# Block-sparse attention and a gated feed-forward on one core: new orders on all engines, with five edits of layout and casts

## The chip, the cores and the metric

The kernel runs on one core of one Trainium2 chip. Five engines work side by side, each through its own list of instructions in order: TensorE (matmuls; PE in the profile, PEld for its weight loads), VectorE (DVE), ScalarE (ACT), GpSimd (POOL) and SyncE (SP, which here only issues DMAs). They wait for each other by semaphores. The metric is the device time of one execution in microseconds (us).

## The reference

Attention first: 4 batches, 8 heads, 768 positions, head size 64. Positions form 24 blocks of 32. A query block sees its own and its two neighbouring blocks, the first and the last block, and three sampled blocks; the first and the last query block see everything. Then x (3072 tokens, 512 wide) goes through a dense feed-forward of width 2048.

```python
scores = scale * np.matmul(q, k.transpose(0, 1, 3, 2))
...
scores = np.where(mask, scores, -1000000000.0)
scores = scores - np.max(scores, axis=-1, keepdims=True)
attn = np.exp(scores)
attn = attn / (np.sum(attn, axis=-1, keepdims=True) + 1e-09)
return np.matmul(attn, v).astype(np.float32)
...
h = x @ w_in
g = h * (1.0 / (1.0 + np.exp(-beta * h)))
return (g @ w_out).astype(np.float32)
```

## The kernel before, in words

The work is cut into 1,731 small tasks. A planner (class `Plan`) gives each an engine and a start, from a list of costs in us, dependencies, priorities and a table of corrections (`OFFSET`); then the tasks are written out in the planned order. So every engine's order is fixed when the program is built, and the costs in the code decide the order, not the result. All matmuls are in f16 with f32 sums in eight PSUM banks.

*Opening, batch 0.* V, K and Q come in halves of four heads as f32 (SP's queue, L528, in the order V, V, K, K, Q, and Q's second half after the store of V). VectorE casts K and Q to f16 (`castK`, `castQ`, L538, two heads at a time, head after head) and V (`vperm0`, L330). TensorE transposes K and Q (`trK`, `trQ`, L632): twelve transposes of 128x64 for a pair of heads, two of them side by side in the array. ScalarE or VectorE copies the result to KT and QT (`evK`, `evQ`, L328, L330, L334, L336). V goes back to memory as a table of rows (`vtab`, L659), from which blocks are fetched.

*A pair of query blocks n (44 of them, eleven a batch).* GpSimd gathers the sampled K blocks to one of three buffers KG (`kg`, L710), the fixed ones come by `kn` on GpSimd or VectorE (L330). The V blocks come by DMA to the buffers VG (`vg`, SP, L810); for the first four pairs the sampled V blocks are picked by one-hot matmuls instead (`pick`, L825, and `pickv`, a copy from PSUM). TensorE makes mask and scores (`sc`, L849 and L862); VectorE takes the maxima (`mx`, L884); ScalarE the exponentials (`ex`, L892); pairs from 11 on are normalized on GpSimd or VectorE (`nrm`, L915), earlier ones get the reciprocals by a matmul (`hl`, L902 to L904 and L953) and a multiply at the end (`rs`, `xv`, L986). TensorE transposes the weights (`tp`, L929), VectorE or ScalarE copies them (`ptv`, L328, L330), TensorE multiplies with V (`av`, L963, L971), and the copy to xT is `xv`. The first and last blocks have their own tasks (`gs`, `gm`, `ge`, `gr`, `gn`, `gt`, `gptv`, `gav`, `gx`, L1026 to L1092).

*Weights.* GpSimd issues w_in as eight DMAs of a quarter of the columns by two row groups (`win`, 2 KB rows, L557) and w_out as eight (`wout`, L563). A one-element copy on GpSimd (`touch`, L543) holds them until V blocks of pair 2 are there.

*Feed-forward.* Eight groups of 8 or 16 blocks (256 or 512 tokens). For each of 16 column tiles f: `h` (TensorE, L1155, four matmuls), `tanh` (ScalarE, L1161), `stt` (VectorE, L1166). Then `y` for each 128 tokens (TensorE, L1182, 16 matmuls in four parts), `oe` to SBUF (ScalarE, L334) and `od` to memory (SP, L1214). These matmuls stand in the order between those of attention and fill TensorE. The very last output is split: ScalarE takes columns 0 to 255, VectorE 256 to 511, then SP and ScalarE issue a store each (L1206).

*Later batches* are loaded by GpSimd (`ldV`, `ldK`, `ldQ`, L588), already as f16.

Of the kernel before, what the change touches and what calls it, by code (L numbers as in the profile page):

```python
# [10 lines left out]
FP32 = mybir.dt.float32  # L11
# [12 lines left out]
class Task:  # L24
    def __init__(self, name, eng, dur, emit, deps=(), prio=0.0, lat=0.0,
                 opens=(), closes=(), moe=False, dma=0.0, slack=0.0, hw=0, bulk=None):
        self.on = {eng: dur} if isinstance(eng, str) else dict(eng)
        self.name, self.eng, self.dur, self.emit = name, None, None, emit
        self.deps = [d for d in deps if d is not None]
# [4 lines left out]
        self.tiling = Plan.TILING.get(self.kind, 0)  # L34
        self.end = None


class Plan:


    HOP = 0.18
# [23 lines left out]
    def run(self):  # L65
# [16 lines left out]
        ring_at = hw_at = 1.0  # L82
        lanes = [0.0] * 8
        issued = 0

        tiling = 0
# [24 lines left out]
        while done < len(tasks):  # L111
            progress = False
            for e in engines:
# [104 lines left out]
def kernel(  # L218
# [472 lines left out]
    for n, (b, p) in enumerate(order_pairs):  # L691
# [287 lines left out]
        if wide:  # L979
            av[n].tiling = 0  # L980
# [277 lines left out]
```

## Time and profile before

| what | us |
|---|---|
| median of 3 runs | 302.6 |
| the runs | 302.6, 358.62, 301.27 |
| span of the profiled execution | 302.9 |
| busy: TensorE, VectorE, ScalarE, GpSimd | 279.5, 237.5, 218.6, 170.0 |
| last matmul starts its last group of eleven at | 295.75 |

How to read the lines: the page gives the busy time of each engine; *stretches* give it for chosen pieces of the span, with the TensorE clock that was granted (1.00 is full) and the mean busy share of the 16 DMA engines. A row of the *timeline* has start, duration, engine, line, operation, what it writes and reads, and how many such instructions are merged; in brackets stands the idle time before it and who ended that. A row of *groups* has busy time and mean ns of one, then the idle time before them. The row of a DMA has its issues, the size of each, and the median time from issue to landing.

### The profile page before, as it was taken

Reading aid. Unit: us, or ns where it says so; the run is one execution under the profiler, and the core shown is the slowest. Engines: PE = TensorE matmul, PEld = TensorE weight load, DVE = VectorE, ACT = ScalarE, POOL = GpSimd, SP = SyncE. Lnnn points to the kernel's source line nnn. Section 1 sums busy time; section 2 is a strip of 40 time slices with the busy share of each in tenths; the row PEclk is TensorE's granted clock in tenths of the full one; section 3 lists DMA queues with packets and bytes.
Section 4 is the critical chain, followed back from the end, with each engine's and each line's share of the span. In section 5 each row is a group of like instructions: output and inputs, shape, how many; then the busy total and the mean of one; then the engine's idle time right before and its main releaser. Section 6 shows DMA issues by size and latency. Waiting matters only on the chain.

```text
span 302.9 us, 11451 instructions
## 1 busy us (share of the span) xinstructions
PE 279.5 (92%) x4109; PEld 173.8 (57%) x4109; DVE 237.5 (78%) x556; ACT 218.6 (72%) x641; POOL 170.0 (56%) x513
## 2 busy tenths in 40 slices
PE   2599879999998799999999999999999999999993
PEld 1465668758846576665556555545554544555671
DVE  5848987999899998999999739999888834762150
ACT  3357657888789598799889749896787768763360
POOL 5057995034579957899777538677976654000000
PEclk9999957999999999999999999999999999999999
DMA  7999999979978852299933643248465446541102
GB/s 248 365 294 171 205 232 231 228 142 265 213 126 167 181 192 72 84 173 162 237 99 106 202 154 106 67 110 167 120 158 119 126 106 181 137 121 53 53 36 69
DMA packets 57170, 47.55 MB, mean 157 GB/s; under 512 B 19733, under 2 KB 53142, under 8 KB 57114
## 3 DMA queue, kind: packets, MB, share of 16 engines
q1 hardware_dynamic: 44736, 35.48, 41.3%
q0 software_dynamic: 12320, 11.27, 24.7%
q8 instruction: 32, 0.52, 0.7%
q14 instruction: 24, 0.20, 0.2%
q10 hardware_dynamic: 58, 0.07, 0.1%
HBM read 45.23 MB, written 9.44 MB: 180 GB/s over the span
## 4 chain that ended last, share of the span: by engine, by line
PE 49%; DVE 23%; issue 7%; ACT 6%; POOL 6%; DMA 5%; POOLq 2%; SPq 0%; DVEq 0%; ACTq 0%
PE bank L1155 17%; PE bank L1182 14%; DVE ST L884 5%; PE bank L825 4%; DVE g L1166 4%; PE bank L929 3%; POOL KG L710 3%; DMA g<-in_k_dram 3%; DVE SG L1040 3%; POOL PP L915 2%; PE bank L963 2%; PE bank L971 2%; ACT PP L892 2%; PE bank L632 2%; ACT t L1161 2%
## 5 line engine op out<-in xcount | busy, mean ns | idle before, releaser
L1155 PE MATMUL bank<-xT,w_in_sb 128*128 128x256 f16 (+1 forms) x512 | 93.8, 330 | 1.5 <-DVE g L1166 1.5
L892 ACT ACTIVATE PP<-bank,ST 128x256 f16<-128x256 f32 x176 | 81.9, 482 | 15.1 <-DVE ST L884 10.1
L1182 PE MATMUL bank<-w_out_sb,g 128*128 128x512 f16 x384 | 92.0, 379 | 0.0
L1161 ACT ACTIVATE t<-bank,beta_sb 128x512 f16<-128x512 f32 (+1 forms) x128 | 71.0, 595 | 15.7 <-PE bank L1155 10.4
L915 POOL TENSOR_SCALAR PP<-PP,ST 128x256 f16<-128x256 f16 x132 | 63.4, 499 | 30.8 <-DVE ST L909 29.2
L1166 DVE SCALAR_TENSOR_TENSOR g<-t,bank 128x512 f16<-128x512 f16 (+1 forms) x128 | 67.0, 547 | 16.3 <-ACT t L1161 15.8
L1155 PEld LDWEIGHTS <-w_in_sb 128*128 128x128 f16 x512 | 54.4, 115 | 28.1 <-issue 4.1
L710 POOL COPY KG<-KT 128x64 f32 x264 | 52.4, 249 | 25.6 <-PE bank L862 10.5
L884 DVE TENSOR_REDUCE ST<-bank 128x2 f32<-128x512 f32 x88 | 57.6, 680 | 4.2 <-PE bank L862 3.8
L1182 PEld LDWEIGHTS <-g 128*128 128x128 f16 x384 | 35.0, 98 | 37.4 <-issue 3.5
L892 ACT ACTIVATION_READ_ACCUMULATOR PP<-bank,ST 128x1 f32 x176 | 37.4, 212 | 0.0
L1061 POOL TENSOR_SCALAR PG<-PG,SG 128x768 f16<-128x768 f16 x13 | 13.1, 1010 | 24.4 <-ACT PG L1049 15.2
L334 ACT ACTIVATE osb<-bank 128x512 f32<-128x512 f32 (+1 forms) x24 | 14.2, 590 | 16.1 <-PE bank L1182 16.0
L330 DVE COPY PT<-bank 128x1024 f16<-128x1024 f16 x30 | 20.4, 683 | 3.8 <-PE bank L929 3.6
L330 DVE CAST xT<-bank 64x256 f16<-64x256 f32 (+1 forms) x35 | 14.6, 418 | 9.9 <-PE bank L963 6.8
L929 PE MATMUL bank<-identity,PP 128*128 128x128 f16 x248 | 20.4, 225 | 1.2 <-ACT KT L328 0.6
L963 PEld LDWEIGHTS <-VG 128*128 128x128 f16 x448 | 16.1, 98 | 9.2 <-issue 4.3
L1049 ACT ACTIVATE PG<-bank,SG 128x384 f16<-128x384 f32 x32 | 18.3, 589 | 4.2 <-DVE SG L1042 3.6
L929 PEld LDWEIGHTS <-PP 128*128 128x128 f16 x248 | 16.2, 101 | 6.0 <-issue 1.1
L963 PE MATMUL bank<-PT,VG 128*128 128x64 f16 x448 | 17.5, 193 | 2.2 <-DMA PT<-PP 1.5
L330 POOL COPY KG<-KT 128x384 f32<-128x384 f32 (+3 forms) x43 | 16.6, 411 | 1.3 <-PE bank L862 1.3
L328 ACT CAST xT<-bank 64x256 f16<-64x256 f32 (+1 forms) x30 | 11.3, 375 | 8.2 <-PE bank L1089 3.9
(119 smaller groups left out, 317.9 us busy)
## 6 DMA issues: line engine op xcount, KB each, us to landing
VG<-VT SPq DMA_DIRECT2D x220, 32.0 KB, 2.6
VG<-VT SPq DMA_DIRECT2D x32, 192.0 KB, 2.7
out_dram<-osb SPq DMA_DIRECT2D x20, 256.0 KB, 2.1
RV<-in_v_dram POOLq DMA_DIRECT2D x6, 384.0 KB, 6.6
RK<-in_k_dram POOLq DMA_DIRECT2D x6, 384.0 KB, 6.2
VT<-Vn SPq DMA_DIRECT2D x3, 768.0 KB, 3.4
RQ<-in_q_dram POOLq DMA_DIRECT2D x6, 384.0 KB, 6.3
w_in_sb<-in_moe_w_in_dram POOLq DMA_DIRECT2D x8, 256.0 KB, 8.8
```

The source lines that it names most:

```text
L330: (nc.vector if eng == "DVE" else nc.gpsimd).tensor_copy(out=out, in_=in_)
L710: nc.gpsimd.tensor_copy(out=kg32[:, g, :, (SR + r) * W:(SR + r + 1) * W], in_=kt32[:, :, bass.ds(vals[3 * g + r], W)])
L884: mx[n, u] = add(f"mx{n}.{u}", "DVE", 0.6, lambda n=n, u=u, sb_=sb_: nc.vector.tensor_reduce(out=sb_[:, 0, 2 * u:2 * u + 2], in_=bank(("S" ...
L892: nc.scalar.activation(out=pb[:, u, g, :], in_=bank(("S", n, u))[:, g * 256:(g + 1) * 256], func=AF.Exp, bias=sb_[:, 0, 2 * u + g:2 * u + ...
L915: (nc.vector if eng == "DVE" else nc.gpsimd).tensor_scalar(out=pb[:, u, g, :], in0=pb[:, u, g, :], scalar1=sb_[:, 2, 2 * u + g:2 * u + g + ...
L929: nc.tensor.transpose(out=o[:, s * P:(s + 1) * P], in_=pb[:, u, g, c * P:(c + 1) * P], identity=identity)
L963: nc.tensor.matmul(o[:, (g * NHP + hp) * 2 * BLK:(g * NHP + hp + 1) * 2 * BLK], lhsT=vgb[:, g, c, hp * P:(hp + 1) * P], rhs=pt[:, g, c, :, ...
L1049: nc.scalar.activation(out=pg[:, :].rearrange("x (j p) -> x j p", j=J)[:, :, hf * hw_:(hf + 1) * hw_], in_=bank(("GS", m, hf))[:, 0:S // 2 ...
L1155: nc.tensor.matmul(o[:, 0:TW], lhsT=w_in_v[:, c, f // 4, f % 4, :], rhs=xT[:, c, c0:c0 + TW], start=(c == 0), stop=(c == NHP - 1))
L1161: lambda G=G, f=f, TW=TW, tt=tt: nc.scalar.activation(out=tt[:, 0:TW], in_=bank(("H", G, f))[:, 0:TW], func=AF.Tanh, bias=0.0, scale=beta_ ...
L1166: lambda G=G, f=f, TW=TW, tt=tt, gg=gg: nc.vector.scalar_tensor_tensor(out=gg[:, f, 0:TW], in0=tt[:, 0:TW], scalar=1.0, in1=bank(("H", G, ...
L1182: nc.tensor.matmul(o[:, :], lhsT=gg[:, f, s * P:(s + 1) * P], rhs=w_out_sb[:, f, :], start=(f == 0), stop=(f == N_FFC - 1))
```

## The change

Five edits by hand and new orders:

- batch 0's casts write the two heads of a pair side by side, so that one 128x128 transpose serves both (6 for a pair of heads in place of 12); a cast may go to ScalarE;
- the V buffers hold the two halves of the keys apart (half, slot, block, column in place of slot, block, half, column);
- w_in comes as eight DMAs of one row group by half of the columns (4 KB rows); an h tile waits for the four DMAs of its half;
- the last output is scaled whole by ScalarE;
- up to ten f32 matmuls on constants are put into gaps of TensorE that the plan expects before 50 us (`emit_spare`);
- the planner's costs are set anew, it counts TensorE's instructions in blocks, `OFFSET` has some 550 entries for single tasks, and `FORCE` fixes the engine of some tasks.

```diff
-    HOP = 0.18
+    HOP = 0.14
+    NI = {"selb": 4, "rows": 8, "maskb": 2, "betaT": 8, "pick": 12, "trK": 24, "trQ": 24, 
+          "sc": 48, "tp": 16, "gs": 32, "gt": 12, "gav": 96, "h": 8, "y": 8}
+    BLOCK, FRONT, FIRST, SLOW, FAST, EASY = 256, 300, 448, 6.9, 2.6, 60.0
...
+        for t in tasks:
+            if t.name in self.FORCE:
+                t.on = {self.FORCE[t.name]: t.on[self.FORCE[t.name]]}
...
+                if e == "PE":
+                    wait = self.SLOW if now < self.EASY else self.FAST
+                    if coming is not None and coming <= now:
+                        got, coming = got + self.BLOCK, None
+                    had += t.ni
+                    while had > got:
+                        coming = now + wait if coming is None else coming
+                        t.dur = max(t.dur, coming - now)
+                        got, coming = got + self.BLOCK, None
+                    if coming is None and had > got - self.FRONT:
+                        coming = now + t.dur + wait
...
-    VGs = sb("VG", [P, NVG, 2, 2, D_MODEL])
+    VGs = sb("VG", [P, 2, NVG, 2, D_MODEL])[:, :, :, :, :].rearrange("x c n g m -> x n g c m")
...
+    mixed = lambda t: t[:, :, :].rearrange("p h x -> p (h x)").rearrange("p (j m) -> p j m", j=J)
...
-                    f"cast{nm}0.{hp}", "DVE", 0.5,
-                    lambda i=i, dst=dst, hp=hp: nc.vector.tensor_copy(
-                        out=dst[:, 2 * hp:2 * hp + 2, :], in_=stage32(i, hp)),
+                    f"cast{nm}0.{hp}", {"DVE": 0.48, "ACT": 0.74}, None,
+                    lambda eng, i=i, dst=dst, hp=hp: copy_on(
+                        eng, mixed(dst)[:, :, hp * P:(hp + 1) * P].rearrange("p j (u d) -> p u j d", u=2),
+                        stage32(i, hp).rearrange("p u (j d) -> p u j d", j=J)),
...
+    for f in range(2):
+        fs = slice(f * D_FF // 2, (f + 1) * D_FF // 2)
+        for c in range(NHP):
+            t_win.append(add(f"win{f}.{c}", "POOL", 0.6, lambda c=c, fs=fs: nc.gpsimd.dma_start(
+                out=w_in_sb[:, c, fs], in_=w_in_r[:, c, fs]),
+                deps=[touch[f]], prio=-50 + 0.4 * f + 0.05 * c, dma=1.5, bulk=THR))
...
+                    if b == 0:
+                        for j in range(J):
+                            nc.tensor.transpose(out=o[:, j * P:(j + 1) * P],
+                                                in_=mixed(s16)[:, j, hp * P:(hp + 1) * P], identity=identity)
+                        return
...
-            th = add(f"h{G}.{f}", "PE", 4 * (TW / 2400.0 + 0.003), emit_h, deps=xdeps + t_win[f // 4 * 2:f // 4 * 2 + 2],
+            th = add(f"h{G}.{f}", "PE", 4 * (TW / 2400.0 + 0.003), emit_h, deps=xdeps + t_win[f // 8 * NHP:f // 8 * NHP + NHP],
...
-                te.emit, te.on = lambda ob=ob, G=G, s=s: scale_on(
-                    "ACT", ob[:, 0:256], bank(("Y", G, s))[:, 0:256], 0.5), {"ACT": 0.35}
-                tf = add(f"of{G}.{s}", "DVE", 0.35, lambda ob=ob, G=G, s=s: scale_on(
-                    "DVE", ob[:, 256:512], bank(("Y", G, s))[:, 256:512], 0.5), deps=list(te.deps), prio=te.prio,
-                    closes=(("Y", G, s),))
...
+    tiny = ones[:, :].bitcast(FP32)
+    spare, at_ = {}, 1.6
+    for t in order:
+        if t.eng != "PE":
+            continue
+        gap = t.start - at_
+        each = 0.86 if t.start < COLD else 0.43
+        k = int(FILL * gap / each)
+        if k and t.start < UNTIL:
+            calm = [(max([z for a, z in h if a < t.start - 1e-9] + [0.0]), i) for i, h in enumerate(held_at)]
+            z, i = min(calm)
+            if z < at_ + 0.1:
+                spare[t] = (i, k)
+        at_ = t.start + t.dur
+    def emit_spare(i, k):
+        for _ in range(k):
+            nc.tensor.matmul(banks[i][0:D, 0:256], lhsT=tiny, rhs=tiny.rearrange(
+                "x (a m) -> x a m", a=1).to_broadcast([P, 4, D]), start=True, stop=True, skip_group_check=True)
```

The built orders differ from the first instruction on. In the opening TensorE's order was sc0 sc1, sc2, tp0 tp1, av0 av1, tp2, sc3 sc4 sc5, av2, sc6, tp3, sc7, tp4, av3, tp5, av4, h0.0; it is now sc0 sc1 sc2, sc3, tp1 tp2 tp0, av1, sc4, av0, sc6, av2, sc7, tp4 tp3, sc5, av3, gs0, av4, tp5, then h0.7, 0.3, 0.2, 0.4, 0.5, tp7, h0.1, 0.0, 0.6, sc8, gt0, av5, y0.1.0, h0.9. GpSimd's was kg0 to kg2, the touches, four w_in, kg3 kg4, w_in, kn4, w_in, kg5, two w_in, kn6, kg6 kg7, then w_out and kg8 to kg10 in turn; it is now kg0 to kg2, a touch, two w_in (0.2, 0.1), kg3, kn4 kn5, two touches, three w_in (0.0, 0.3, 1.0), kg4, w_in 1.3, w_out, kg6 kg7, w_out, kn7, kg5, kg9, kn10, w_out, kg8, w_out, kg10, two w_out, w_in 1.1 and 1.2, two w_out.

More of the change, by code (lines that the diff above doesn't have):

```diff
@@ L165, in run @@
                         hw_at = begin + took
-                        end = lanes[issued % 8] = hw_at + 0.9 + (self.LATER if ring_at > hw_at else 0.0)
+                        end = lanes[issued % 8] = hw_at + 1.4 + (self.LATER if ring_at > hw_at else 0.0)
                         issued += 1
@@ L553 @@
     THR = 4.5
-    for fq in range(4):
-        fs = slice(fq * FQ * P, (fq + 1) * FQ * P)
-        for c in range(0, 4, 2):
-            t_win.append(add(f"win{fq}.{c // 2}", "POOL", 0.6, lambda c=c, fs=fs: nc.gpsimd.dma_start(
-                out=w_in_sb[:, c:c + 2, fs], in_=w_in_r[:, c:c + 2, fs]),
-                deps=[touch[fq // 2]], prio=-50 + 0.2 * fq + 0.05 * c, dma=1.3, bulk=THR))
+    for f in range(2):
[4 more added lines that the diff above has]
+                deps=[touch[f]], prio=-50 + 0.4 * f + 0.05 * c, dma=1.5, bulk=THR))
     for c in range(4):
@@ L920 @@
         if not late:
-            nrm[n] = add(f"nrm{n}", {"POOL": 1.85, "DVE": 0.8}, None, emit_nrm, deps=[rc], prio=pr - 0.5)
+            nrm[n] = add(f"nrm{n}", {"POOL": 1.6, "DVE": 0.8}, None, emit_nrm, deps=[rc], prio=pr - 0.5)
         def emit_tp(n=n, pb=pb):
@@ L1226 @@
     order = plan.run()
+    held_at = [[] for _ in range(8)]
+    shut = {}
+    for t in order:
+        for name in t.closes:
+            shut[name] = max(shut.get(name, 0.0), t.end)
+    for t in order:
+        for name in t.opens:
+            held_at[plan.bank[name]].append((t.start, shut[name]))
+    tiny = ones[:, :].bitcast(FP32)
+    spare, at_ = {}, 1.6
+    for t in order:
+        if t.eng != "PE":
[13 more added lines that the diff above has]
+                "x (a m) -> x a m", a=1).to_broadcast([P, 4, D]), start=True, stop=True, skip_group_check=True)
     with tc.manual_schedule():
         for t in order:
-            t.emit(t.eng) if len(t.on) > 1 else t.emit()
+            if t in spare:
+                emit_spare(*spare[t])
+            t.emit(t.eng) if t.many else t.emit()
 _INS = ['q', 'k', 'v', 'sampled_blocks', 'moe_w_in', 'moe_w_out', 'moe_beta']
```

101 lines of the change are left out of this document (54 added, 47 removed).

## The prediction, before the changed kernel was run

> **What bounds the kernel now.** I read the page's busy shares and clock line first, then the busy time of each engine stretch by stretch, then the timeline of the stretch that stands out.
>
> ```profile
> span 302.9 us, 11451 instructions
> PE 279.5 (92%) x4109; PEld 173.8 (57%) x4109; DVE 237.5 (78%) x556; ACT 218.6 (72%) x641; POOL 170.0 (56%) x513
> PEclk9999957999999999999999999999999999999999
> q8 instruction: 32, 0.52, 0.7%
> ```
>
> The share of TensorE (92%) hides stages. Stretches, with columns length, then PE, PEld, DVE, ACT, POOL busy (instructions), granted clock, DMA share, GB/s:
>
> ```profile
> 0.00:15.00 15.00, 5.85 (x60) 4.12 (x61) 10.04 (x34) 5.44 (x8) 3.85 (x24) 1.00 0.90 306
> 15.00:20.00 5.00, 5.00 (x40) 3.06 (x39) 3.21 (x12) 2.10 (x3) 4.37 (x18) 1.00 1.08 327
> 20.00:25.00 5.00, 5.00 (x88) 2.94 (x87) 1.83 (x3) 2.60 (x5) 0.44 (x4) 1.00 1.09 235
> 25.00:30.00 5.00, 5.00 (x58) 2.98 (x57) 4.86 (x14) 4.72 (x20) 4.99 (x15) 1.00 0.92 144
> 30.00:35.00 5.00, 5.00 (x206) 4.05 (x205) 4.49 (x12) 2.63 (x10) 5.00 (x14) 1.00 1.19 190
> 35.00:40.00 5.00, 2.04 (x58) 1.13 (x56) 4.90 (x11) 4.65 (x20) 4.87 (x23) 0.87 1.17 233
> 40.00:45.00 5.00, 5.00 (x112) 4.28 (x98) 4.26 (x13) 2.19 (x10) 4.34 (x17) 0.50 1.15 230
> 45.00:50.00 5.00, 5.00 (x68) 3.95 (x67) 3.20 (x10) 3.83 (x14) 4.42 (x9) 0.61 1.08 236
> 50.00:90.00 40.00, 40.00 (x707) 28.45 (x705) 37.89 (x103) 32.78 (x99) 14.82 (x41) 1.00 1.01 199
> 90.00:120.00 30.00, 26.37 (x576) 19.43 (x573) 28.60 (x61) 25.24 (x79) 24.06 (x70) 1.00 0.66 155
> 120.00:160.00 40.00, 39.89 (x620) 23.80 (x619) 39.20 (x90) 34.76 (x110) 34.65 (x96) 1.00 0.73 147
> 160.00:260.00 100.00, 97.08 (x1305) 53.15 (x1303) 78.25 (x169) 78.39 (x235) 64.20 (x190) 1.00 0.51 133
> 260.00:298.00 38.00, 38.00 (x251) 22.42 (x249) 16.30 (x32) 18.91 (x36) 0.00 (x0) 1.00 0.26 76
> ```
>
> Four stages are to be seen. Up to 50 us attention opens, no engine is full throughout, and the clock is halved from 40. From 50 to 160 VectorE paces: 37.89 of 40, 28.60 of 30, 39.20 of 40, while TensorE stands idle 3.63 us in 90 to 120. From 160 to 260 TensorE paces (2.92 idle). From 260 to 298 it has no idle time at all. So 1 us won on VectorE before 160 counts nearly whole, provided that MoE matmuls are then ready; in the last stage nothing can be won.
>
> ```profile
> 37.11 0.25 PE L849 MATMUL bank<-maskr,ones 64*32 64x192 f16 x1
> 39.54 0.36 PE L849 MATMUL bank<-maskr,ones 64*32 64x192 f16 x7 [2.17 <-DVE ST L884]
> ```
>
> TensorE stops inside a run of eight equal mask matmuls: one starts at 37.11, seven at 39.54. The view puts 2.17 us down to a reduction, but the place fits another cause: in the built order the stopped pair is TensorE's 960th and 961st instruction of 8,216, and the page shows 32 instruction packets of 0.52 MB, about one for 257 instructions. I take it for a late packet of code. After it the clock is 0.50 to 0.61 for 10 us.
>
> The Trainium skill, TensorE: Matmul & The Clock Gate, Part 1, says that an idle window of about 3.4 us halves the clock and a busy one restores it. The 0.50 after the gap agrees; that TensorE shows 5.00 of 5 busy in 40 to 45 and stays halved does not fit a 3.4 us recovery, and the row decides.
>
> **The change, part by part.**
>
> ```profile
> 21.21 0.86 PE L632 MATMUL bank<-identity,RQ 128*64 128x128 f16 x24
> 49.42 0.61 PE L929 MATMUL bank<-identity,PP 128*128 128x128 f16 x8
> L538 DVE CAST RK<-g 128x768 f16<-128x768 f32 x4 | 2.1, 555 | 0.8 <-DMA g<-in_k_dram 0.8
> L328 ACT COPY KT<-bank 128x768 f16<-128x768 f16 x12 | 9.6, 817 | 6.4 <-PE bank L632 6.4
> L330 DVE COPY KT<-bank 128x768 f16<-128x768 f16 x4 | 3.8, 946 | 0.0
> L330 DVE CAST xT<-bank 64x256 f16<-64x256 f32 x34 | 14.2, 418 | 9.7 <-PE bank L963 6.8 <-ACT xT L328 2.4
> L330 DVE COPY KG<-KT 128x256 f16<-128x256 f16 x16 | 3.8, 277 | 0.1
> L1061 DVE TENSOR_SCALAR PG<-PG,SG 128x768 f16<-128x768 f16 x3 | 1.9, 640 | 0.0
> L330 DVE COPY PT<-bank 128x1024 f16<-128x1024 f16 x30 | 20.4, 683 | 3.8 <-PE bank L929 3.6
> L328 ACT COPY PT<-bank 128x1024 f16<-128x1024 f16 x1 | 1.0, 1020 | 0.0
> L915 POOL TENSOR_SCALAR PP<-PP,ST 128x256 f16<-128x256 f16 x132 | 63.4, 499 | 30.8 <-DVE ST L909 29.2
> ```
>
> *Opening casts.* 96 half-width transposes of batch 0 become 48 full ones. Before: 0.86/24 = 0.036 each, 3.4 us; now 0.61/8 = 0.076 as an upper bound, 3.7 us. TensorE time: -0.7 to +0.3, taken 0. What matters is 96 instructions fewer (a weight load goes with each matmul), so the code delivered up to any moment reaches further into the work. The strided casts cost 0.555 on VectorE (no row shows the stride; 0.555 to 0.95, since 0.946 is its dearest 768-column copy), about 0.82 on ScalarE. Five of eight go to ScalarE.
>
> *Moves between engines, counted in the two built orders.* VectorE loses 10 PT copies (10 x 0.683 = 6.8) and 5 casts (2.8), and gains 4 KT copies (3.8), 2 Q scalings (about 1.9, as KT) and 12 normalizing multiplies of 128x256. The latter have no VectorE row: 0.277 by a copy of their size, 0.640 by a multiply of three times the size; 3.3 to 7.7, taken 0.3 each, 3.6, by the row of the same size. Some twenty small copies go either way at about 0.4 (the xT row) and cancel within 1.5. Sum: -6.8 - 2.8 + 3.8 + 1.9 + 3.6 = -0.3, ends -2.1 to +5.3: taken 0. ScalarE gains 10 x 1.020 + 5 x 0.817 and loses 6 x 0.817: about 9.4 over the span; it has 7 us free in 50 to 90 and 10 in 90 to 160, so this hides if it is spread. GpSimd loses 12 x 0.499 = 6.0.
>
> *SP's queue.* The loads go V, Q, V, K, K instead of V, V, K, K, Q, so that Q's first half is cast and transposed while K still flies. The second V half, and with it the store of V and everything behind it (Q's second half, the VG reads, the touch on GpSimd that lets w_in start), stands one load later: 0.79 MB at 306 GB/s, 2.6 us. The queue is full to 25 us (share 0.90, then 1.08), so these transfers wait in it anyway; 0 to 2.6 us late, taken 0.5, which is inside the opening's term below.
>
> *New orders.* Most of the effect is here. In the opening three score groups stand together, the transposes after them, and by the 960th TensorE instruction eight score groups are issued instead of six. VectorE's idle time from 15 to 50 is 1.79 + 3.17 + 0.14 + 0.51 + 0.10 + 0.74 + 1.80 = 8.25; this bounds the gain. The loads keep some 3 us of it (1.79 and most of 3.17 lie before the last Q half is there). I take 5.0. In 90 to 160 TensorE idles 3.74; VectorE is nearly full, so I take 1.5. In 160 to 260, 2.92 idle; I take half, 1.5. Each could be lost again, as the order is new everywhere; ends: a loss of 2 (another gap as that at 37.11) to 8.25, 3.7 and 2.9.
>
> ```profile
> L557 POOL DMA_DIRECT2D w_in_sb<-in_moe_w_in_dram x8 | 5.9, 743 | 0.6 <-POOL w_out_sb L543 0.5
> L563 POOL DMA_DIRECT2D w_out_sb<-in_moe_w_out_dram x8 | 4.1, 518 | 0.0
> w_in_sb<-in_moe_w_in_dram POOLq DMA_DIRECT2D x8, 256.0 KB, 8.8
> 38.84 1.12 POOL L710 COPY KG<-KT 128x64 f32 x6
> 13.99 1.94 PE L825 MATMUL bank<-Vn,xT 128*96 128x512 f16 x4
> ```
>
> *w_in in 4 KB rows.* Eight issues of 0.743 us stay eight; bytes are equal. Landing was 8.8; with rows twice as long between half of it and the same, taken 8.8. But h tiles of a half now wait for four transfers, where a quarter waited for two.
>
> *V buffers with halves apart, ten spare matmuls.* The transfers keep count, bytes and row length on the memory side: 0, with up to 1 us either way in an opening that moves data all the time. Eight of the spares stand ahead of the first pick, while TensorE waits for data; the trace has none of their type (f32, 256 columns). Low end: f16 of 256 columns, 0.61/8 x 2 = 0.15; high end: an early pick of 512 columns, 1.94/4 = 0.49, twice over for operands of twice the bytes, 0.97 (an estimate). Ten cost 1.5 to 9.7 us of idle time; the code fills 0.7 of each gap that it expects, so at the high end one group is some 1 us late. Taken 0.
>
> ```profile
> 298.33 0.38 ACT L334 ACTIVATE osb<-bank 128x256 f32<-128x256 f32 x1 [2.86 <-PE bank L1182]
> 298.74 0.42 DVE L336 TENSOR_SCALAR osb<-bank 128x256 f32<-128x256 f32 x1 [6.39 <-ACT osb L334]
> 299.20 0.33 SPq L1206 DMA_DIRECT2D out_dram<-osb  x1
> 294.87 0.60 ACT L334 ACTIVATE osb<-bank 128x512 f32<-128x512 f32 x1 [2.98 <-PE bank L1182]
> ```
>
> *One-engine last output.* The two halves ran one after the other: 298.33 to 299.16. One whole costs 0.60: -0.23, wholly on the path.
>
> Sum: 5.0 + 1.5 + 1.5 + 0.2 = 8.2 off the profiled 302.9, which is 0.1% over the median shown (302.6): 294.7. I lower this to **294.0**, since the clock's half rate (work of 10 us at about 0.55) is partly on TensorE's account as well.
>
> **Rivals.** *All idle time comes back*: 8.25 + 3.7 + 2.9 + 0.2 = 15.0: 287.9, or 287. For it: the gap at 37.11 and the halved clock have one cause that the new order spaces out. Against: VectorE is full from 50 on.
>
> *GpSimd paces the opening instead.* It is busy 4.99, 5.00, 4.87, 4.34, 4.42 of 5 from 25 to 50, and the gather of a pair is 1.12. The new order issues five gathers (kg3 to kg7) with six w_in and two w_out between them, so score groups come no earlier. Opening 0, rest 3.2: 299.7. Against: the old order issued eight w_in in the same place.
>
> *The second half of w_in is late; slower.* Two of its four transfers stand on GpSimd behind kg8, kg10 and six w_out. From the release of kg8 (the end of score group 5): 2 x 1.12 + 3 x 0.518 + 2 x 0.743 = 5.3, plus 8.8 to land: 14.1 us. From there to the first tile that needs them (h0.9, after eight others) VectorE has 40 instructions in its order, at the mean of 35 to 50 (12.36/34 = 0.364) 14.6 us. So the cover just suffices. Each us of landing beyond 9.3 stops TensorE, in order, with attention's next groups behind it; 5 us late halves the clock again (10 us at 0.55: some 4 us), and with the opening's gain gone: 302.9 - 3.2 + 5 + 4 = 308.7. It makes the kernel slower from about 4 us late.
>
> *Code is not what stops TensorE.* The gap is then the attention chain's, which the new order keeps: the opening gives 1 at most: 302.9 - 1 - 3.2 = 298.7. Against: the gap inside a run of equal instructions.
> The Trainium skill states this rule: Runtime: NRT & Kernel Launch, Instruction fetch mechanics, has code come in 16 KiB blocks of 256 instructions, fetch hidden. The packets agree in size; the gap at 37.11 speaks against hidden.
>
> **Chances.** Forecast (290 to 298) 0.52; all idle back (286 to 290) 0.17; GpSimd paces (297 to 301) 0.13; code hidden (298 to 300) 0.05; w_in late (303 to 311) 0.13. Range 286 to 302: it leaves out the late w_in and little else. Two per cent, about what a measurement of this kernel tells from no change, is 296.5 and 308.7. Faster: 0.17 and 0.49 of the forecast's, 0.66. Slower: 0.08 of the late w_in's. Same: 0.26.
>
> **What would show it.**
>
> ```profile
> 46.06 0.47 ACT L1161 ACTIVATE t<-bank,beta_sb 128x256 f16<-128x256 f32 x1 [0.58 <-PE bank L1155]
> ```
>
> Right: no half clock after 35 us; VectorE over 4.5 of 5 in each stretch from 25; first tanh before 44 instead of 46.06; TensorE idle in 90 to 120 under 2.5 us; last store 0.2 us closer to the last matmul. Wrong: a wait of h for w_in; gathers of KG as the last releaser of scores; ScalarE full where VectorE was; a new gap of over 1 us on TensorE in a run of equal instructions.

## The result and the profile after

| what | before | after |
|---|---|---|
| median of 4 runs each on one chip, us | 302.47 | 317.24 (314.69 to 318.91) |
| ratio | | 1.0486, 95% interval 1.04 to 1.0572 |
| span of the profiled execution, us | 302.9 | 314.3 |

The kernel is 4.9% slower. One of before's four runs took 358.62 us, in a slower state that the ratio leaves out. The page of after, the lines that answer to before's:

```profile
span 314.3 us, 11323 instructions
PE 283.1 (90%) x4081; PEld 174.3 (55%) x4081; DVE 235.4 (75%) x566; ACT 227.2 (72%) x653; POOL 163.7 (52%) x490
PEclk9999799999999999999999999999999999979998
q8 instruction: 32, 0.52, 0.7%
```

The engines' sums came out within the ends that were counted: VectorE 2.1 us less, ScalarE 8.6 more, GpSimd 6.3 less. What was lost is time in which TensorE waits. The stretches of after, columns as in the prediction:

```profile
25.00:30.00 5.00, 3.88 (x71) 1.89 (x53) 4.42 (x8) 4.39 (x19) 2.73 (x9) 1.00 0.53 100
30.00:35.00 5.00, 4.63 (x137) 3.59 (x130) 4.66 (x15) 4.32 (x15) 5.00 (x18) 1.00 1.04 184
35.00:40.00 5.00, 3.85 (x103) 2.88 (x103) 3.25 (x11) 2.84 (x13) 4.20 (x21) 0.66 1.09 199
40.00:45.00 5.00, 2.98 (x88) 1.66 (x85) 3.92 (x8) 4.40 (x15) 3.48 (x16) 1.00 1.09 254
45.00:50.00 5.00, 3.57 (x73) 3.23 (x66) 4.79 (x16) 4.03 (x17) 4.39 (x13) 1.00 0.89 157
50.00:90.00 40.00, 36.77 (x673) 27.68 (x672) 33.90 (x95) 29.59 (x80) 14.14 (x36) 1.00 1.00 197
90.00:120.00 30.00, 26.54 (x572) 18.82 (x569) 28.56 (x67) 26.50 (x85) 23.99 (x63) 1.00 0.71 146
160.00:260.00 100.00, 92.45 (x1299) 51.79 (x1305) 77.67 (x174) 76.07 (x232) 55.72 (x171) 1.00 0.54 138
260.00:298.00 38.00, 35.91 (x276) 19.10 (x274) 16.37 (x36) 18.69 (x40) 5.20 (x10) 0.96 0.31 80
```

TensorE's idle time, plus what a lower clock cost it (busy time times one less the clock), summed by stage over stretches of 5 us (the last one as long as the trace has it). Up to 25 us the spare matmuls count as busy, so that stage is left out. The later rows belong to the experiments:

```
span of the trace     25-50  50-90  90-160  160-260  260-end   sum
before        302.9    7.7    0.0     3.7      2.9      4.6   18.9
after         314.3    7.4    3.2     3.6      7.6      8.2   30.0
e3, SP tail   312.8    6.3    7.3     3.5      5.5      5.3   27.9
e10           305.4    6.2    1.0     5.2      5.2      4.5   22.1
e14           305.3    6.4    1.4     5.0      4.1      4.4   21.3
e13           299.8    7.4    0.0     1.9      2.2      4.4   15.9
e12           306.9   10.1    1.0     1.6      5.5      4.8   23.0
e5            303.1   10.3    0.0     1.6      3.5      4.6   20.0
e16           302.3    7.1    0.0     3.5      2.4      4.7   17.7
e17           302.4    8.1    0.0     1.5      3.8      4.6   18.0
e19           305.9    8.7    0.0     3.5      5.0      4.4   21.6
```

After loses 30.0 - 18.9 = 11.1 of its 11.4 us more span here: 3.2 in 50 to 90, none in 90 to 160, 4.7 in 160 to 260, 3.6 behind that. In 25 to 50 before had a stop and a halved clock, 7.7 in all; after has other stops instead, 7.4. Next to nothing was won there.

What TensorE waited for from 200 us on, in after (us in total, times, longest), then in before:

```profile
PE bank L997 <- DMA PT<-PP: 5.3, 3, 3.0
PE bank L997 <- DMA VG<-VT: 2.1, 1, 2.1
```

```profile
PE bank L963 <- DMA PT<-PP: 1.5, 3, 0.7
```

SyncE's queue at that time, in after and then in before: start, duration and count of what it issued. The rows `VG<-VT` are gathers of V blocks (`vg`), `PT<-PP` are transposes.

```profile
231.04 1.30 SPq L967 DMA_TRANSPOSE PT<-PP  x1
232.44 13.37 SPq L843 DMA_DIRECT2D VG<-VT  x23
245.91 1.28 SPq L967 DMA_TRANSPOSE PT<-PP  x1
...
267.42 5.40 SPq L843 DMA_DIRECT2D VG<-VT  x11
```

```profile
223.18 5.24 SPq L810 DMA_DIRECT2D VG<-VT  x9
228.53 1.24 SPq L933 DMA_TRANSPOSE PT<-PP  x1
...
234.00 4.52 SPq L810 DMA_DIRECT2D VG<-VT  x7
238.63 1.26 SPq L933 DMA_TRANSPOSE PT<-PP  x1
```

In the last third SyncE also transposes the weights (`tpd`, by DMA). Its queue has little slack there: from 180 to 275 us it waited some 12 us for other engines, in before 16, and a gather costs it 13.37/23 = 0.58 us, the reading of its addresses included. In after `tpd37` stands behind 23 gathers, 12 of which are for pairs 39 and 40. It was issued at 245.91. Its weights had been normalized by 231.67:

```profile
229.82 1.85 POOL L949 TENSOR_SCALAR PP<-PP,ST 128x256 f16<-128x256 f16 x4 [2.89 <-DVE ST L943]
```

TensorE, in order, on the product with V of pairs 37, 40 and 42:

```profile
248.80 0.63 PE L997 MATMUL bank<-PT,VG 128*128 128x64 f16 x16 [3.05 <-DMA PT<-PP]
...
258.47 0.64 PE L997 MATMUL bank<-PT,VG 128*128 128x64 f16 x16 [0.94 <-DMA PT<-PP]
...
273.79 1.09 PE L997 MATMUL bank<-PT,VG 128*128 128x64 f16 x32 [2.09 <-DMA VG<-VT]
```

After the last of these the clock was 0.66 from 275 to 280 us, with TensorE busy for 5.00 of 5: 1.7 of the 8.2 us behind 260.

### The profile page after: what moved, and what is told of

Same layout as the page of the kernel before. It is cut to its first block, busy times and chain, and to the rows that moved or that the text cites. A ratio compares the mean times of both kernels' runs of the same rounds, so it can differ in the third digit from the quotient of the medians.

```text
span 314.3 us, 11323 instructions
## 1 busy us (share of the span) xinstructions
PE 283.1 (90%) x4081; PEld 174.3 (55%) x4081; DVE 235.4 (75%) x566; ACT 227.2 (72%) x653; POOL 163.7 (52%) x490
## 5 line engine op out<-in xcount | busy, mean ns | idle before, releaser
L1216 PE MATMUL bank<-w_out_sb,g 128*128 128x512 f16 x384 | 90.6, 380 | 0.0
L743 POOL COPY KG<-KT 128x64 f32 x264 | 53.2, 250 | 42.0 <-PE bank L895 19.5
L949 POOL TENSOR_SCALAR PP<-PP,ST 128x256 f16<-128x256 f16 x120 | 58.1, 502 | 30.0 <-DVE ST L943 29.9
L358 ACT ACTIVATE osb<-bank 128x512 f32<-128x512 f32 x24 | 14.3, 603 | 19.4 <-PE bank L1216 19.2
L997 PEld LDWEIGHTS <-VG 128*128 128x128 f16 x448 | 15.6, 98 | 16.5 <-issue 10.5
L354 DVE CAST xT<-bank 64x256 f16<-64x256 f32 (+1 forms) x31 | 13.0, 419 | 13.3 <-PE bank L997 12.4
L895 PE MATMUL bank<-KG,QT 64*32 64x256 f16 x704 | 17.5, 276 | 2.9 <-issue 1.6
L963 PE MATMUL bank<-identity,PP 128*128 128x128 f16 x248 | 18.7, 221 | 0.0
L963 PEld LDWEIGHTS <-PP 128*128 128x128 f16 x248 | 15.4, 98 | 5.3 <-issue 0.5
L352 ACT CAST xT<-bank 64x256 f16<-64x256 f32 (+1 forms) x34 | 12.6, 372 | 5.3 <-PE bank L997 4.1
L1075 DVE TENSOR_REDUCE SG<-bank 128x1 f32<-128x384 f32 x32 | 16.2, 547 | 0.2 <-PE bank L1061 0.2
```

The costliest lines, as they stand in the source:

```text
L743: nc.gpsimd.tensor_copy(out=kg32[:, g, :, (SR + r) * W:(SR + r + 1) * W], in_=kt32[:, :, bass.ds(vals[3 * g + r], W)])
L895: nc.tensor.matmul(bk[u][hp * BLK:(hp + 1) * BLK, g * 256:(g + 1) * 256], lhsT=QT[b % 2][u * D:(u + 1) * D, hp, (i0 + g) * BLK:(i0 + g + 1 ...
L949: (nc.vector if eng == "DVE" else nc.gpsimd).tensor_scalar(out=pb[:, u, g, :], in0=pb[:, u, g, :], scalar1=sb_[:, 2, 2 * u + g:2 * u + g + ...
L963: nc.tensor.transpose(out=o[:, s * P:(s + 1) * P], in_=pb[:, u, g, c * P:(c + 1) * P], identity=identity)
L997: nc.tensor.matmul(o[:, (g * NHP + hp) * 2 * BLK:(g * NHP + hp + 1) * 2 * BLK], lhsT=vgb[:, g, c, hp * P:(hp + 1) * P], rhs=pt[:, g, c, :, ...
L1216: nc.tensor.matmul(o[:, :], lhsT=gg[:, f, s * P:(s + 1) * P], rhs=w_out_sb[:, f, :], start=(f == 0), stop=(f == N_FFC - 1))
```

## The experiments

Three theories stood at the start. *Orders on SyncE*: gathers and transposes issued late stop TensorE. *GpSimd*: its order, with the third gather of K behind w_in, delays the opening. *Layouts*: the casts, the V buffers or the rows of w_in cost the time, whatever the order. Later a fourth came up, *instruction packets*. Medians are in us, each with the ratio to before on the same chip and its 95% interval.

**e1: the four layout edits in before's kernel; before's planner sorts anew.** The edit is the diff above without the planner, the tables and the spares.

> The kernel before with the four layout edits (casts with heads side by side on either engine and their 128-column transposes, V buffers with key halves apart, w_in in 4 KB rows, one-engine last output), no spare matmuls, and the old planner with its old costs and due times. Theory A (the re-planned orders cost the 14.8 us between 302.5 and 317.2; the layouts are neutral): 298 to 306 us, no wait of several us late in the span (the scores-times-values stages in 240 to 285 wait under 3 us in sum). Rival B (a layout costs it: the strided casts, the V halves or the wider w_in pieces): 309 to 318 us. Rival C (the ten spare matmuls cost it): as A, and then the next run falls by as much.

308.05, 1.0177 (1.0129 to 1.0225). A part of the loss, 5 of 14.8 us, comes without the new orders. But the planner had also moved tasks, so the layouts are not yet separated from an order.

**e2: after without the spares.**

```diff
-FILL = 9.0, 50.0, 0.7
+FILL = 9.0, 50.0, 0.0
```

> The changed kernel without its ten spare matmuls, all else and all orders as they are. Theory A (orders): 314 to 320 us, the spares being worth -1 to +2 us; if they keep the clock up, the half clock after 36 us gets longer, from 0.66 mean in 35 to 40. Rival C (the spares cost it): 303 to 312 us.

318.28, 1.0551 (1.0478 to 1.0624), against after's 1.0486. The single runs, 313.41 to 321.74, lie on both sides of after's: the spares neither cost nor bring anything that shows.

**e3: after, with six entries of SyncE's queue moved ahead.**

```diff
+    for name, ahead in (("vg37.1", "vg37.2"), ("tpd37", "vg38.2"), ("vg39.2", "vg39.3"),
+                        ("vg39.4", "vg39.5"), ("vg41.4", "vg41.5"), ("vg42.2", "vg42.3")):
+        place(name, ahead)
```

> The changed kernel with six entries of the SP queue moved up in the last 90 us, nothing else moved: the gathers vg37.1, vg39.2, vg39.4, vg41.4 and vg42.2 each beside the other gathers of its pair, and the DMA transpose tpd37 two places behind the stage that frees its buffer. Theory A1 (SyncE's queue holds back what TensorE needs: TensorE waited 3.0 us ahead of av37, 1.1 ahead of av38 to av40 together with it, 2.1 ahead of av42): those waits go, 310 to 312.5 us. Rival D (GpSimd's normalization or the gathers' landing is as late and takes their place): 315 to 318 us.

313.29, 1.0341 (1.03 to 1.0383): about 4 us of the loss, with no other edit. The waits of 3.05 and 2.09 are gone, though shorter ones for transposes stay (six, the longest 1.8). From 160 us on the loss falls from 15.8 to 10.8. In 50 to 90 this trace loses 7.3, 2.5 of them by a lower clock, since there another gather was late:

```profile
58.20 0.61 PE L1005 MATMUL bank<-PT,g 128*64 128x32 f16 x16 [3.57 <-DMA g<-VT]
```

That is `vg5.5`, issued at 51.23 and landed at 58.06; twelve gathers of later pairs stand between it and the one of its own pair ahead of it. In after the same matmuls waited only 1.26 us, so this place differs by 2 us between executions of one order.

**e4: after, with kg3 ahead of w_in on GpSimd.**

```diff
+    place("kg3", "touch0")
```

> The changed kernel with one GpSimd task moved: the key gather kg3 ahead of the touch and the two w_in transfers instead of behind them. GpSimd stood idle from 24.13 to 27.11 ahead of the first w_in transfer with no semaphore to wait for. Theory E (an instruction packet of GpSimd comes late; one of 8 KB ran at 25.06 to 25.58): kg3 gets the gap instead and still starts at 26.5 to 27.5; time 316 to 318.5. Rival F (the issue of the transfer itself waits): kg3 starts at 24.8 to 25.3, the fourth scores stage at 26 to 27 in place of 28.07 to 30.07, 314.5 to 316 us.

316.12, 1.0445 (1.0398 to 1.0492), which can't be told from after's. The view of GpSimd in after shows what was to be removed:

```profile
23.95 0.18 POOL L569 COPY w_in_sb<-VG 1x1 f16<-1x1 f16 x1
27.11 1.33 POOL L583 DMA_DIRECT2D w_in_sb<-in_moe_w_in_dram  x2 [2.98 <-issue]
28.59 1.12 POOL L743 COPY KG<-KT 128x64 f32 x6
```

It stands 2.98 us, with no semaphore to wait for, ahead of its first w_in, and kg3 starts at 28.59. In e4 kg3 started at 26.51, and the end did not follow it by anything that can be told.

**e5: the four layouts in exactly before's order,** written out task by task.

> The four layout edits in the kernel before with its order of instructions, engines and PSUM banks written out task by task, so that no planner can move anything (e1 gave 308.05 us, but its planner had re-sorted 20 per cent of TensorE's tasks). The eight w_in transfers stand at the same places of GpSimd's queue, the casts stay on VectorE. Theory A (orders alone cost time): 301 to 305 us. Rival B (a layout costs it): 306 to 310 us.

Median 307.05 (304.38 to 310.01), against 301.06 for before. The two fastest, 304.38 and 305.02, lie 3 to 4 us above it. So the layouts lose some 3 to 4 us in before's order as well: not the order alone.

**e6: the reverse, after's order with the old casts, V buffers and 2 KB rows of w_in.**

> The reverse of it: the changed kernel with its order as it is (engines, queues and spare matmuls too), but with the old contents: casts head by head with 64-row transposes, V buffers as before, w_in in 2 KB rows. Theory A: 314 to 320 us, like the changed kernel. Rival B: 308 to 313 us.

323.92, 1.0719 (1.0592 to 1.0845): worse than after. One place:

```profile
57.91 0.62 PE L1184 MATMUL bank<-xT,w_in_sb 128*128 128x256 f16 x2 [7.97 <-DMA w_in_sb<-in_moe_w_in_dram]
```

That is h0.3, the second h tile in the order, and then h0.2. They went on when win1.1 landed (57.87) and when win1.2 did (59.84). They read neither: both pieces hold columns of the other half. But an old piece spans two row groups, and the wait that the build derives seems to cover what lies between its two parts. After's order issues these two pieces late; with rows of 4 KB, one row group to a piece, only h0.8 and later wait for them.

**e7: e3 and four more moves on SyncE, in the opening.**

```diff
+                        ("vg5.5", "vg7.0"), ("vg7.2", "vg8.5"), ("vg7.1", "vg8.5"), ("vg7.3", "vg8.5")
```

> The changed kernel with the six SP entries of e3 moved and four more near the front: the gather vg5.5, which stood behind eleven gathers of later pairs and landed at 54 to 58 us, when TensorE had waited in av5 for 1.4 to 3.9 us in the four traces, goes beside the other gathers of its pair; vg7.1, vg7.2 and vg7.3 go ahead of those of pairs 8 to 10. Theory A1 (the SP order costs it): av5 waits for no gather, 308.5 to 311.5 us against 313.3 of e3. Rival D (the next thing is as late: w_in's second half landed at 56.5 to 58.4, when av5 was over): 312 to 315 us.

310.87, 1.0315 (1.0233 to 1.0398). The interval overlaps e3's, so the gain is not shown by the times. The wait for `vg5.5` is gone from the trace, and what it had covered shows:

```profile
56.92 1.72 PE L1189 MATMUL bank<-xT,w_in_sb 128*128 128x256 f16 x14 [1.46 <-DMA w_in_sb<-in_moe_w_in_dram]
```

This is h0.9 waiting for the second half of w_in, the prediction's slower rival.

**e8: e7, and the transposes of pairs 38 and 39 ahead of five gathers of pair 40.**

```diff
+                        ("vg40.2", "mx41.1"), ("vg40.3", "mx41.1"), ("vg40.4", "mx41.1"),
+                        ("vg40.5", "xv37.1"), ("vg40.6", "xv37.1"), ("od5.0", "xv37.1")
```

> The kernel of e7 with the DMA transposes tpd38 and tpd39 ahead of five of the seven gathers of pair 40, which are wanted 10 us later. In e7 the normalization before tpd38 was done at 242.78, SyncE issued gather after gather without a pause and came to tpd38 at 246.90; TensorE waited 2.15 us for it and ran 0.83 of its clock from 245 to 255. Theory A1 (SyncE's order is what paces the tail): av38 starts 2 to 3 us earlier, 307.5 to 309.5 us against 310.9. Rival D (SyncE's total work paces it, whatever the order: 0.47 us a transfer): the wait moves to av39 or av40, 310 to 311.5.

310.48, 1.0259 (1.0209 to 1.031): no gain over e7. Pair 38 no longer waits, but the next ones do:

```profile
251.13 0.65 PE L997 MATMUL bank<-PT,VG 128*128 128x64 f16 x16 [0.91 <-DMA PT<-PP]
255.56 0.63 PE L997 MATMUL bank<-PT,VG 128*128 128x64 f16 x16 [1.16 <-DMA PT<-PP]
```

Here moving a transpose ahead only moved the wait. That fits a queue whose whole work paces, which no run tested by itself.

**e10: e8, and the two late pieces of w_in ahead of the second w_out on GpSimd.**

```diff
+                        ("win1.1", "wout1.1"), ("win1.2", "wout1.1")
```

> The kernel of e8 with the two last w_in transfers (win1.1 and win1.2) moved up on GpSimd's queue, ahead of the third w_out transfer, kg8, kg10 and two more w_out. In e7 the first product that needs them (h0.9) waited until 56.88 us, 2.0 us. Rival of the prediction (w_in's second half late decides): those 2 us go, 305.5 to 308 if e8 gives 308.5. Theory A1 alone (it only shows once the gather vg5.5 no longer hides it, and DVE's g is as late): 307.5 to 309.

307.73, 1.0157 (1.0122 to 1.0193), 2.75 us less than e8 on the same chip; the intervals do not touch. The wait of h0.9 is gone. This is the price of the late w_in in that order.

**e6b: after with old casts and old V buffers, w_in kept in 4 KB rows.**

> The changed kernel in its own order, with the old casts and 64-row transposes and the old V buffers, but with w_in in its new 4 KB rows. In e6, with 2 KB rows in the same order, the third hidden product waited 8.0 us for w_in pieces of the second half, at 50 to 58 us. If that wait is all that e6 lost (323.9 against 317.2): 315 to 318 us, and casts and V buffers are worth nothing in this order. If they are worth something: 319 to 323.

317.86 (313.49 to 319.27), as after (314.69 to 318.91). Every run of e6 (321.04 to 328.27) lies above every run here. So in after's order the 4 KB rows are worth about 6 us (323.92 to 317.86); the casts and V buffers bring or cost nothing that this spread would show.

**e13: before's exact order with V halves, 4 KB rows and one-engine output, old casts.**

> The kernel before in its exact order with the V halves, the 4 KB rows and the one-engine output, but with its own casts and transposes. e5, with the new casts as well, gave 304.4 to 310.0 us against 301.1. If the casts made that (96 fewer instruction pairs on TensorE ahead of 23 us move the boundaries of its instruction packets into other places): 300 to 303 here. If V halves or w_in made it: 304 to 308.

302.66 (10 runs), 1.0017 (0.9984 to 1.0049). These three edits cost nothing that shows.

**e12: before's exact order with the casts and transposes alone.**

> The kernel before in its exact order with the new casts and the 128-column transposes alone (the casts on VectorE, as there). e13 (V halves, 4 KB rows, one-engine output in that order) was level with before, 1.0017 [0.9984, 1.0049]; e5 (all four) was 304.4 to 310.0. If the casts are what e5 paid: 304 to 310 us here, the loss standing ahead of 60 us. If e5's upper runs were a matter of that chip: 301 to 304.

307.08, 1.0135 (1.0082 to 1.0188). So it is the casts that lose 4.3 us in before's order. Where TensorE stopped, in e12 and then in e13:

```profile
37.17 0.41 PE L869 MATMUL bank<-KG,QT 64*32 64x256 f16 x7 [3.82 <-issue]
```

```profile
33.87 0.30 PE L862 MATMUL bank<-KG,QT 64*32 64x256 f16 x7 [0.77 <-issue]
...
40.76 0.36 PE L849 MATMUL bank<-maskr,ones 64*32 64x192 f16 x7 [3.29 <-DVE HL L903]
```

All three are inside runs of equal matmuls, at TensorE's 705th and 961st instruction (matmuls and weight loads counted in the trace, good to about four), which is 192 and a multiple of 256, plus one. The trace has the packets that bring TensorE's instructions, 16 KB each, as transfers of a queue of their own. "st." and "stop" mark where TensorE stood:

```
us        enters    3rd packet  705th     4th packet  961st
          448th     starts      starts    starts      starts
before    28.7      30.66       33.20     37.32       39.54 stop
e13       28.2      31.44       33.87 st. 38.39       40.76 stop
e12       30.7      34.82       37.17 st. 41.28       44.19
e5        30.1      34.00       36.37 st. 40.36       43.38
after     30.6      33.68       36.15 st. 41.24       43.58 stop
e16       28.9      31.66       34.04     39.14       41.47 stop
e17       29.8      32.24       34.43 st. 39.30       41.50 stop
e18       23.7      25.72       31.90     35.16       37.48 stop
e19       21.9      24.12       31.14     34.58       37.01 stop
```

At every stop TensorE goes on 2.2 to 2.5 us after the packet starts. In these rows the packet starts 2.0 to 5.1 us after TensorE has entered the 256 instructions before. A fixed pace would explain the first seven rows as well, where the fourth packet follows the third by 6.4 to 7.6 us. In e18 and e19, which come below, it follows by 9.4 and 10.5, and 3.3 and 3.4 after the 705th: it goes with TensorE's progress.

The view names VectorE for the stop at the 961st in before, e13 and e16, and the stopped pair does wait for two semaphores. By the counts in the program they stand for a reduction of VectorE, over at 36.80 in before, and an exponential of ScalarE, over at 37.91. TensorE went on at 39.54. In e13 and e16 both were over at 38.25 and 38.51, and it went on at 40.76 and 41.47. So 1.6, 2.5 and 3.0 us of these stops are no wait for another engine.

With 48 transposes fewer TensorE reaches its 192nd instruction later (22.5 us in e12, 19.4 in before), and the second packet (24.58 against 19.73) and the third start later too. What starts the second is not shown: in after and e17, for instance, it came 1.1 to 1.2 us ahead of the 193rd instruction. The 705th is reached as early as ever, at 33.0. TensorE then stands for 3.8 us, and the clock is 0.71, 0.50 and 0.50 in the 15 us from 35. Of the third packet's 4.2 us of lateness 2.0 are the later entry into the 448th; why it then took 2.2 us more to start is not shown. In 25 to 50 e12 loses 2.4 us more than before, and in 160 to 260 another 2.6. e5, whose trace has the same stop (3.55), loses 2.6 and 0.6 there.

**e14: e10's order up to planned 180 us, then before's, without spares.**

> The kernel of e10 up to the fifth gather of pair 31 (planned at 180 us), and from there all tasks that are left in the exact order and on the engines of the kernel before; PSUM banks dealt out anew; no spare matmuls (e2 found nothing in them). e10's trace was 0.3 us behind the one of before with 180 of TensorE's 268 us of work done, and 2.8 behind at the end. Theory A1 (what e10 still loses is the order of the last third): 301.5 to 304.5 us, level with before. Rival (it is in the layouts, or in the splice): 306 to 309.

307.23 (10 runs), 1.0138 (1.0094 to 1.0182), as e10. The PSUM banks were dealt out anew as well. So giving the last third its old order back gains nothing that shows.

**e15: e14 with kg3 first, as in e4.**

> e14 with kg3 ahead of the touch and the first w_in transfers on GpSimd, as in e4, where the wait of 1.5 to 3.0 us ahead of the first w_in transfer was not seen and the fourth scores stage found its keys ready. If kg3 is what holds the opening back: 1 to 2 us under e14, 300 to 303, and the first version under the kernel before. If other waits (instruction packets, VectorE) take its place: level with e14.

309.94, 1.0236 (1.0184 to 1.0287), 2.7 us worse than e14. Its trace stops 2.0 us at the 705th instruction, where e14's doesn't. So kg3's late place on GpSimd is no cause of the loss; the late w_in, on the same queue, is (e10).

**e16: e12 with each of batch 0's 48 transposes issued twice,** so that TensorE's list is as long as before's again.

```diff
+                            for _ in range(2):
                                 nc.tensor.transpose(out=o[:, j * P:(j + 1) * P],
```

> Before's written-out order with the casts and full-width transposes alone, as in the run that took 307.1 us, but each of the 48 transposes of batch 0 is issued twice (the first result is overwritten by an equal one), so that TensorE's list has as many instructions as before's. Theory (the casts lose by where the instruction packets fall): the stop at TensorE's 705th instruction, 4.09 us there, goes back to about 1, the one at the 961st returns (2.4 to 3.5 us), and the time falls to 302 to 304.5, though TensorE has some 2 to 4 us more work in the opening. Rival (the casts themselves, strided and two heads wide, or the full transposes are what costs): 307 or more, since the doubled work is added to it.

303.39 (12 runs), 1.0011 (0.9981 to 1.004), level with before. More work, and 3.7 us faster than e12 (before took 302.73 and 302.74 beside them): the casts' loss is gone, and with it the stop at the 705th. The old stop is back:

```profile
41.47 0.36 PE L857 MATMUL bank<-maskr,ones 64*32 64x192 f16 x7 [3.51 <-DVE HL L912]
```

**e17: only K's 24 transposes twice.**

> The same with only K's 24 transposes issued twice, 48 instructions fewer than before. Theory of the packets: between the two, 303 to 306.5, with a stop at the 705th instruction of 1.5 to 3.5 us. Rival: 307 or more here too.

304.99 (12 runs), 1.0073 (1.0035 to 1.0112): between the two, with a stop of 1.27 at the 705th. 48, 24 and 0 transposes given back make 303.4, 305.0 and 307.1.

**e18 and e19: e13 with 48 or 96 tiny matmuls more at 7.7 us,** where TensorE waits.

```diff
+        for i in range(97):
+            w = NM if i == 96 else 16
+            nc.tensor.matmul(bank("mask")[:, 0:w], lhsT=ones[0:1, :], rhs=mrow[:, 0:w], start=True, stop=True)
```

> Before's written-out order with the V halves, the 4 KB rows and the one-engine output (302.7 us in its own run), and 48 more tiny matmuls ahead of the mask matmul at 7.7 us, where TensorE waits 2.9 us for the first casts; their results are overwritten, the rest is as before. They move TensorE's 192nd, 448th, 704th and 960th instruction 96 places earlier in the work. Theory (a stop comes where the packet of the next 256 instructions starts later than 2.3 us ahead of the place that needs it): the second packet starts soon after the mask instead of at 19 to 20 us, the third near 25, the fourth near 32, so that neither the 705th nor the 961st instruction waits; the stop of 2.4 to 3.5 us goes, perhaps the half clock after it, and the time is 298 to 301. Rival (the stop hides another wait of the same length, or VectorE takes the time back): the gap stays in the trace or the time stays at 302 to 303.5.

> The same with 96 such matmuls, 192 places. Theory: the places of need fall at before's 512th and 768th instruction and the packets start in time; a stop of some 0.6 us at the 1217th is possible, as packets follow each other by 6.1 us; 298 to 301.5. If the added matmuls themselves outlast the wait of 2.9 us, the opening is up to 3 us later: 301 to 304. Rival: 302 to 304, with the old stop still there.

e18: 304.06 (12 runs), 1.0025 (0.9988 to 1.0062). e19: 306.19, 1.0113 (1.0069 to 1.0158). The theory had forecast 298 to 301 and no stop at the 961st, and failed in both. The stop at the 705th is gone in both, but the one at the 961st stayed, now 192 instructions earlier in e19's work:

```profile
37.01 0.27 PE L852 MATMUL bank<-maskr,ones 64*32 64x192 f16 x7 [3.15 <-issue]
```

The fourth packet was expected as soon as TensorE passes its 704th (31.1); it started 3.4 us later. In this part of e19 256 instructions take TensorE 2.4 us, less than the packet's delay, so these two additions moved the stop and did not remove it. e19's loss, 3.2 us, is seen in 25 to 50 (8.7 against e13's 7.4), in 90 to 160 (3.5 against 1.9) and in 160 to 260 (5.0 against 2.2).

## Why the prediction was wrong

294.0 us was forecast, in a range of 286 to 302, and 317.24 came.

*The opening, -5.0: failed.* From 25 to 50 us after loses 7.4 us, before 7.7. The stop at 39.54 was read rightly as code that comes late, for 1.6 of its 2.17 us. The step that failed is "96 instructions fewer [...], so the code delivered up to any moment reaches further". The row of 37.11 and 39.54 showed a late packet, not that packets come at fixed times. In the traces they go with TensorE's own progress, and with fewer instructions ahead of them they came later. The cast term, taken at 0 with ends of -0.7 and +0.3, cost 4.3 us in before's order. The prediction also read six score groups ahead of before's stop and eight in after's order. The traces have seven in before (112 score matmuls of 16 a group) and 7.8 in after, so less than one group was to be won. The casts as such were priced rightly, as the rows of after show: the stride costs VectorE nothing, ScalarE takes 0.83. So were the multiplies (0.308 each, taken 0.3).

```profile
L354 DVE CAST RK<-g 128x768 f16<-128x768 f32 x2 | 1.1, 552 | 0.0
L352 ACT CAST RK<-g 128x768 f16<-128x768 f32 x2 | 1.7, 833 | 1.7 <-DMA g<-in_k_dram 1.7
L949 DVE TENSOR_SCALAR PP<-PP,ST 128x256 f16<-128x256 f16 x12 | 3.0, 308 | 0.1
L583 POOL DMA_DIRECT2D w_in_sb<-in_moe_w_in_dram x8 | 4.6, 577 | 3.0 <-issue 3.0
w_in_sb<-in_moe_w_in_dram POOLq DMA_DIRECT2D x8, 256.0 KB, 7.6
```

In after's order the casts and V buffers cost nothing that shows (e6b). Its stops are shorter, 1.33 us at the 705th and 1.57 at the 961st:

```profile
36.15 0.19 PE L1005 MATMUL bank<-PT,VG 128*64 128x32 f16 x1 [1.33 <-issue]
...
43.58 0.29 PE L895 MATMUL bank<-KG,QT 64*32 64x256 f16 x3 [1.57 <-issue]
```

The Trainium skill, Runtime: NRT & Kernel Launch, Instruction fetch mechanics, has a block fetched while the one before is executed, and the cost mostly hidden. That the fetch goes with the progress agrees with the packets' times here; that it is hidden does not, in a stretch where a block of 256 lasts 2.4 us (e19).

*SyncE's queue, 0.5 us: failed, and of the steps that were tried in after's order this is the dearest.* It was priced for the loads of the opening alone. The diff's new orders changed the queue to the end of attention, where SyncE has little slack, and the prediction quoted no row of it. Putting six entries back gives 4 us (e3). The rest of SyncE's moves and w_in's together give 5.6 more (e3 313.29 to e10 307.73), 2.75 of them by w_in alone.

*90 to 160 and 160 to 260, -1.5 each: failed.* The first stage lost 3.6 us as before did 3.7, since VectorE stayed full (28.56 of 30). The second lost 7.6 in place of 2.9. "Each could be lost again" was priced at a loss of 2 us, one more gap like that at 37.11. After loses 4.7 us more than before in this stage and 3.6 behind it; six entries of SyncE's queue, put back, give 5.0 of that (e3).

*The late second half of w_in: right as a mechanism, mis-sized.* It was to give 308.7 as the only loss. Its price is 2.75 us (e8 to e10), and in after it lay under the wait for `vg5.5`: TensorE got to h0.9 at 57.6, when the piece landed (57.70). No halved clock followed there.

*GpSimd paces: not borne out.* Scores did wait for KG (0.89 and 0.23 us at 29 to 30 us), but e4, with kg3 first, gained nothing certain and e15 lost.

*Right:* the engines' sums; V halves, 4 KB rows and the last output together at 0 (e13); ten spares at 0 (e2); the 9 us on ScalarE hidden. 4 KB rows in after's order bring more than the 0 taken, some 6 us; with 2 KB rows (e6) h tiles of the first half waited 8 us for the late pieces. The last output went from 298.33 to 299.20, 0.87 us, to

```profile
309.97 0.60 ACT L358 ACTIVATE osb<-bank 128x512 f32<-128x512 f32 x1 [2.86 <-PE bank L1216]
310.59 0.33 SPq L1235 DMA_DIRECT2D out_dram<-osb  x1
```

0.62: -0.25, as against -0.23.

*Of the signs named:* the half clock after 35 was shorter (0.66 in one stretch) but there; VectorE was under 4.5 of 5 in three of five stretches from 25; the first tanh came at 49.76 and not before 44; TensorE idled 3.46 in 90 to 120. New stops of over 1 us and the wait for KG, both named as wrong signs, are there.

*What stays open.* e10 and e14 are still 4 to 5 us slower than before. Their traces lose 22.1 and 21.3 against 18.9: no more than before in 25 to 50, but 1.0 to 1.4 more in 50 to 90, 1.3 to 1.5 more in 90 to 160 and 1.2 to 2.3 more in 160 to 260. In 105 to 110 both ran at a clock of 0.66. A late opening may be what is paid from 160 on: e12 and e19 lose more there too (5.5 and 5.0), with before's own order in that stage. That was not tried by itself. Nor was the cause of GpSimd's 2.98 us settled: in each trace with such a gap an 8 KB packet of another instruction queue starts some 2 us before the gap ends (25.06, and 27.11 in after), which is only argued from the times. No version here beats before; e13, e16 and e18 are level with it.

## What to carry to other kernels

When a change re-sorts an in-order queue with little slack, go through that queue entry by entry, DMAs too: TensorE stood 3 us for one transpose behind gathers of later pairs, and six such entries cost 4. Where TensorE runs through hundreds of tiny matmuls, count its instructions as well as its work: leaving out 48 matmuls cost 4.3 us, and issuing them twice gave it back. Test a layout in the old order, written out, before judging it with a new one.

## What the runs showed of the hardware

- TensorE's instruction packets follow its progress. In the twenty traces the third and the fourth started 1.3 to 5.1 us after it entered a block of 256. At the stops tabled above TensorE went on 2.2 to 2.5 us after the packet's start.
- A stop of 3.8 us inside the score matmuls was followed by a clock of 0.50 for 10 us (e12, 40 to 50), in which TensorE was busy for 9.4. After a wait of 2.09 us (after, 273.79) it was 0.66 for 5 us.
- SyncE needed 0.49 to 0.58 us for a gather of 32 KB and about 1.3 for a transposing DMA; 23 gathers held it for 13.37 us, at a busy share of the DMA engines of 0.41.
- A cast from f32 with its output in pieces of 64 columns cost VectorE 0.552 us, without them 0.555.
